# Moving ScalarE's V copy and, every second turn, a set of TensorE transposes in a fused top-k attention and SwiGLU kernel

## The chip, the core and the metric

The kernel runs on one core of a Trainium2 chip. A core has five engines with an instruction queue each: TensorE (PE in the profile, its weight loads shown apart as PEld), VectorE (DVE), ScalarE (ACT), GpSimd (POOL) and SyncE (SP), which here only starts DMA transfers. They meet through semaphores. PE writes to PSUM, a memory of eight banks, from which ACT or DVE must copy the result before the bank can be used again.

The metric is the time of one execution on the device in microseconds (us). The kernel before was timed three times: median 1794.11 us, from 1790.79 to 1795.02.

## What is computed

Top-k attention over 8 batches of 8 heads with 576 tokens of 64 features each, and a SwiGLU feed-forward block on its output, all in fp32. Cut to what matters:

```python
scores = q @ k.T / sqrt(64)                  # 576 x 576 per head
kth    = 32nd largest score of each row
scores = where(scores >= kth, scores, -1e9)
attn   = exp(scores - max);  attn = attn / (sum(attn) + 1e-9)
x      = (attn @ v), heads side by side      # 4608 x 512
out    = (silu(x @ w_gate) * (x @ w_val)) @ w_out   # 512 -> 1536 -> 512
```

## The kernel before

**Units and turns.** The attention is cut into 160 units: for each of 8 batches, five blocks of queries (four of 128, then one of 64), and in each four pairs of heads. A unit of a full block holds two heads (a score tile of 128 x 1152); one of the last block packs 64 queries of both heads into one tile of 128 x 576. The main loop makes one turn per unit (and three more to drain). In turn n several units are in work at different stages, each stage with a line of the listing:

- DVE picks the 32 largest scores of unit n in rounds of eight (`select`, L328 and L332), then writes a penalty for the others (L338). Last in the turn comes the reciprocal of the sums of the unit n-1, whose exp ran in this turn (`normalize`, L371).
- POOL adds penalty and scores of unit n-1 (`penalize`, L348 and L350).
- ACT takes exp of unit n-1 with the row sums (`weigh`, L359 and L364), and scales the unit before it, n-2, by the reciprocal (the rest of `normalize`, L374; the main loop calls it `scaled`).
- PE transposes unit n-2, nine 128 x 128 pieces or five in a one-head unit, into three PSUM banks or two, and ACT copies them to `et` (`turn`, L386 and L387).
- In even turns alone PE computes the scores of units n+1 and n+2 (`scores`, L308, or L294 for one-head units), which ACT copies to `sc` (L313, L299), and between the two the products of `et` with V for units n-4 and n-3 (`values`, L420), which ACT copies to `x` (L436): the V copy. Even turns thus have much attention work on PE, odd turns only the transposes.

The five PSUM banks of the pool `ps_t` go round among scores, products with V, transposes, and the transposes of K and Q (`prep`, L255 to L268).

**The FFN.** The tokens are taken in 18 blocks of 256 (`feed`). A block can begin when all heads of its tokens are in `x`. Its work on PE is handed out in pieces: four 128 x 256 products, each run as two matmuls in fp32 (L476, eight matmuls for one piece), and later pieces of six matmuls for the output product (L562; L522 in the first block). When a product is complete, work for ACT is put on a list `on_act` (tanh, half and add for a gate, L501 to L503; a plain copy for a value, L508) and from there work for POOL on a list `on_pool` (L504, L509). The lists are emptied by `flush` at fixed places of a turn, or by `piece` when they hold more than one entry. The products go round three PSUM banks of the pool `ps_f`.

**Order.** Every engine runs its instructions strictly in the order in which the program writes them: at the end an order dependency is put between each instruction and the one before it on its engine. How many pieces a turn gets follows from a credit (`share`); where in the turn they stand is written out by hand with `pieces(k)`. So the order of calls in the body of the main loop sets everything around the change.

In that body, a turn begins with `flush(on_act)`, `penalize`, `flush(on_pool)`; then comes the scaling (L374), then in even turns the first scores, the products with V and their copy, the second scores on PE, then exp, then the copies of the second scores. Two pieces follow on PE, `flush(on_act)`, and the transposes with their copies, and then the rest of the pieces.

Of the kernel before, what the change touches and what calls it, by code (L numbers as in the profile page):

```python
# [25 lines left out]
def kernel(  # L26
# [174 lines left out]
    def rounding(n):  # L201
        for _ in range(n):
            next(weight, None)
# [70 lines left out]
    def n_heads(qt):  # L274

        return 1 if qt == J else 2

    def scores(n):
        b, qt, hp = units[n]
        slab = preps[b * NHP + hp]  # L280
        sc = work.tile([P, 2 * S], FP32, tag="sc", name="sc", bufs=3)
        halves = [slice(0, D), slice(D, P)]
        half = S // 2

        def bank():
            return ps_t.tile([P, 512], FP32, tag="t", name="s")


        if qt == J:
            banks = [bank() for _ in range(2)]  # L290
            for i, ps in enumerate(banks):
                for d in halves:
                    k0 = R + i * half
                    nc.tensor.matmul(  # L294
                        ps[d, 0:half], slab[d, S + R : S + 2 * R], slab[d, k0 : k0 + half]
                    )
            yield
            for i, ps in enumerate(banks):
                nc.scalar.copy(sc[:, i * half : (i + 1) * half], ps[:, 0:half])  # L299
        else:  # L300
            q0 = S + 2 * R + qt * P
            banks = []
            for i in range(2):
                for hh, d in enumerate(halves):
                    ps = bank()
                    banks.append((i + 2 * hh, ps))
                    k0 = (1 - hh) * R + i * half
                    nc.tensor.matmul(  # L308
                        ps[:, 0:half], slab[d, q0 : q0 + P], slab[d, k0 : k0 + half]
                    )  # L310
            yield
            for i, ps in banks:
                nc.scalar.copy(sc[:, i * half : (i + 1) * half], ps[:, 0:half])  # L313
        state[n] = dict(sc=sc)

    def select(n):

        nh = n_heads(units[n][1])
        sc = state[n]["sc"]
        m = small.tile([P, 2, TOP_K], FP32, tag="m", name="m", bufs=2)  # L320
        heads = [slice(t * S, (t + 1) * S) for t in range(nh)]
        e = work.tile([P, 2 * S], FP32, tag="e", name="e", bufs=3)
        state[n] |= dict(m=m, e=e, heads=heads)
        cur = sc
        rounds = TOP_K // 8
        for r in range(rounds):
            for t, hs in enumerate(heads):
                nc.vector.max(m[:, t, 8 * r : 8 * r + 8], cur[:, hs])  # L328
                yield
            if r < rounds - 1:  # L330
                for t, hs in enumerate(heads):
                    nc.vector.match_replace(  # L332
                        e[:, hs], m[:, t, 8 * r : 8 * r + 8], cur[:, hs], LOWEST
                    )
                    yield
                cur = e
        for t, hs in enumerate(heads):
            nc.vector.tensor_scalar(  # L338
                e[:, hs], sc[:, hs], m[:, t, TOP_K - 1 : TOP_K], FAR, ALU.is_lt, ALU.mult
            )  # L340
# [26 lines left out]
    def normalize(n):  # L367
        st = state[n]
        tot, e, heads = st.pop("tot"), st["e"], st.pop("heads")
        nh = len(heads)  # L370
        nc.vector.reciprocal(tot[:, 0:nh], tot[:, 0:nh])  # L371
        yield
        for t, hs in enumerate(heads):
            nc.scalar.mul(e[:, hs], e[:, hs], tot[:, t : t + 1])  # L374

    def turn(n):

        last = units[n][1] == J
        e = state[n].pop("e")
        et = work.tile([P, 2 * J + 1, P], FP32, tag="et", name="et")  # L380
        for c0, cn in ((0, J), (J, 1)) if last else ((0, J), (J, 1), (J + 1, J)):
            ps = ps_t.tile([P, 512], FP32, tag="t", name="etps")
            kl = R if last and c0 == J else P
            for c in range(cn):
                k0 = (c0 + c) * P
                nc.tensor.transpose(ps[0:kl, c * P : (c + 1) * P], e[:, k0 : k0 + kl], ident[:])  # L386
            nc.scalar.copy(  # L387
                et[0:kl, c0 : c0 + cn, :],
                ps[0:kl, 0 : cn * P].rearrange("p (c j) -> p c j", c=cn),
            )  # L390
            if c0 == J:
                yield
        state[n]["et"] = et
# [64 lines left out]
    def flush(queue):  # L458
        while queue:
            queue.pop(0)()  # L460
# [201 lines left out]
    NU = len(units)  # L662
# [3 lines left out]
    def piece():  # L666

        if len(on_act) > 1:
            flush(on_act)
        if len(on_pool) > 1:  # L670
            flush(on_pool)
        while True:
            if not current:
                if not todo or done.get(todo[0], 0) < NHP * BLK:
                    return 0
                flush(on_act)
                flush(on_pool)
                current.append(feed(todo.pop(0)))
            cost = next(current[0], 0)
            if cost == 0:  # L680
                current.pop()
                continue
            return cost

    def fetch(n):

        b, qt, hp = units[n]
        i = b * NHP + hp
        if qt == 0:
            yield from prep(i)  # L690
        if qt == J and i + NHP < len(pairs):
            load(i + NHP)

    def share(n):


        others = 0.0
        costs = [(m, 0.7) for m in scored(n) + valued(n)] + [(n - TURN, 0.6)]
        for m, cost in costs:
            if m >= 0:  # L700
                others += cost * (0.5 if units[m][1] == J else 1)
        if units[n + 3][1] == 0:
            others += 0.6

        beside = 6.4 if T[1] else 7.0
        return beside * n_heads(units[n][1]) / 2 - others

    def scored(n):

        ahead = [n + 1] if n < 2 else [] if n % 2 else [n + 1, n + 2]  # L710
        return [m for m in ahead if m < NU]

    def valued(n):

        behind = [] if n % 2 else [n - 4, n - 3]
        return [m for m in behind if 0 <= m < NU]

    def pieces(n):
        for _ in range(n):
            if credit[0] >= 1:  # L720
                credit[0] -= piece()

    def run(steps):
        for _ in steps:
            pass

    def finish_units(ns):
        values(ns)
        for n in ns:
            b, qt, hp = units[n]  # L730
            if qt == J and b + 1 < B:
                load_v((b + 1) * NHP + hp)
# [10 lines left out]
    no = iter(())  # L743
    scaled = no
    TURN = 2
    due = [2.0]
    for n in range(NU + 3):
        nh = n_heads(units[n][1]) if n < NU else 1
        topk = select(n) if n < NU else no
        norm = normalize(n - 1) if 0 <= n - 1 < NU else no  # L750
        nxt = [scores(m) for m in scored(n)]
        ahead = fetch(n + 3 if n else 2) if n + 3 < NU else no

        def dve(k, beside=True):

            for _ in range(k * nh):
                next(topk, None)
                due[0] += 5 / 6 if beside else 0
                if due[0] >= 1:
                    due[0] -= 1  # L760
                    rounding(1)

        if n >= NU - NHP:
            credit[0] = 8.0
        else:
            credit[0] = min(credit[0] + share(n), share(n) + 1)
        flush(on_act)
        if 0 <= n - 1 < NU:
            penalize(n - 1)
        flush(on_pool)  # L770
        run(scaled)
        if nxt:
            run(nxt.pop(0))
        if valued(n):
            finish_units(valued(n))
        if nxt:
            next(nxt[0])
        early[0]()
        if 0 <= n - 1 < NU:
            weigh(n - 1)  # L780
        if nxt:
            run(nxt.pop())


        dve(2, beside=False)
        if n == 0:
            run(ahead)
            load(3)
            ahead = fetch(3)
        if n < NHP:  # L790
            load_v(n)
        pieces(2)
        flush(on_act)
        dve(1)
        dve(1)
        if 0 <= n - TURN < NU:
            run(turn(n - TURN))

        flush(on_pool)
        next(ahead, None)  # L800
        pieces(1)
        next(ahead, None)
        dve(1)
        pieces(1)
        dve(2, beside=False)
        run(topk)
        next(norm, None)
        scaled = norm
        pieces(6)
# [50 lines left out]
```

## Time and profile before

| What | Value |
|---|---|
| median of three runs | 1794.11 us |
| the profiled execution's own time | 1794.33 us |
| its span, first to last instruction | 1792.1 us |
| mean granted PE clock | 0.964 |
| PE busy | 1691.1 us, 94% of the span |
| PE weight loads | 1398.6 us, 78% |
| DVE busy | 1619.1 us, 90% |
| ACT busy | 1204.8 us, 67% |
| POOL busy | 1043.2 us, 58% |
| HBM read and written | 48.23 MB and 9.44 MB, 32 GB/s |
| scaling on ACT (L374), each | 780 ns, 288 of them |
| exp on ACT (L359), each | 775 ns, 288 |
| transposes' copies (L387), each | 483 ns, 448 |
| V copy (L436), each | 328 ns, 96 |

Times in the profile are in us from the span's start unless marked ns. The profile gives each instruction's start and duration; a wait is put down to the instruction whose semaphore came last. The ends of PE's matmuls are modelled, so that small pauses inside PE's busy time do not show. Busy shares are means over the span, and this kernel has a start and an end that differ from its middle.

### The profile page before, as it was taken

To read this page: it belongs to the slowest core of one execution; us is meant where nothing else is said; L and a number is where in the kernel's file an instruction comes from. 1 tells how busy PE (TensorE), PEld (TensorE's weight loads), DVE (VectorE), ACT (ScalarE), POOL (GpSimd) and SP (SyncE) were. 2 spreads that over 40 slices of the span, in tenths; PEclk is the share of its full clock that TensorE was granted. 3 is DMA by queue.
4 is the path that set the end of the run, shared out by engine and by line. 5 is a ranking of instruction groups with operands and counts; after the bars stand their busy time and mean duration, and the time that the engine had idled before them with its cause. 6 is when DMAs were issued, how large, how long until landed. Compare 5 with 4: busy or idle time off the path is not lost.

```text
span 1792.1 us, 30800 instructions
## 1 busy us (share of the span) xinstructions
PE 1691.1 (94%) x11012; PEld 1398.6 (78%) x11012; DVE 1619.1 (90%) x3372; ACT 1204.8 (67%) x2881; POOL 1043.2 (58%) x930
## 2 busy tenths in 40 slices
PE   4558999799999999999999999999999999999999
PEld 3337678688888888888888878888887878888877
DVE  7999999999999999998999999998999989999400
ACT  6778676667667676667666675767676676676431
POOL 4878756455565646565556546555556555656434
PEclk7569999899999999999999999999999999999989
DMA  7433130001200030001200020000300020000000
GB/s 193 128 94 94 32 75 14 13 1 36 60 1 13 2 81 14 13 1 32 64 13 1 13 70 26 1 13 4 92 1 13 1 49 21 13 1 13 1 12 12
DMA packets 109305, 59.66 MB, mean 33 GB/s; under 512 B 88544, under 2 KB 96992, under 8 KB 109152
## 3 DMA queue, kind: packets, MB, share of 16 engines
q1 hardware_dynamic: 108016, 57.37, 12.3%
q8 instruction: 87, 1.43, 0.3%
q14 instruction: 66, 0.54, 0.1%
q10 hardware_dynamic: 1136, 0.33, 0.1%
HBM read 48.23 MB, written 9.44 MB: 32 GB/s over the span
## 4 chain that ended last, share of the span: by engine, by line
PE 79%; DVE 12%; ACT 4%; POOL 3%; issue 1%; DMA 1%; SPq 0%; ACTq 0%; POOLq 0%; DVEq 0%
PE f L476 40%; PE x_ps L562 8%; PE av L420 8%; PE s L308 7%; PE etps L386 6%; PE y_ps L562 5%; DVE m L328 5%; DVE e L332 5%; PE s L294 2%; DVE e L338 1%; PE kqps L263 1%; PE o_ps L522 1%; ACT e L359 1%; POOL e L350 1%; DVE size L121 1%
## 5 line engine op out<-in xcount | busy, mean ns | idle before, releaser
L328 DVE MAX8 m<-e 128x8 f32<-128x576 f32 x864 | 614.9, 747 | 3.3
L350 POOL TENSOR_TENSOR e<-e,sc 128x1152 f32<-128x1152 f32 (+1 forms) x160 | 382.9, 2393 | 131.6 <-DVE tot L371 110.0
L332 DVE MATCH_REPLACE8 e<-m,e 128x576 f32<-128x576 f32 x576 | 423.5, 741 | 0.0
L476 PE MATMUL f<-xT,wg 128*128 128x256 f32 x1728 | 403.9, 383 | 0.0
L476 PE MATMUL f<-xT,wv 128*128 128x256 f32 x1728 | 399.6, 380 | 0.0
L476 PEld LDWEIGHTS f<-xT,wg 128*128 128x128 f32 x1728 | 325.2, 192 | 52.0 <-issue 9.2
L476 PEld LDWEIGHTS f<-xT,wv 128*128 128x128 f32 x1728 | 323.0, 190 | 49.1 <-issue 7.9
L504 POOL TENSOR_TENSOR h<-h,half_g 128x512 f32<-128x512 f32 x108 | 139.7, 1293 | 284.8 <-ACT h L503 283.0
L359 ACT ACTIVATE e<-e,bias 128x576 f32<-128x576 f32 x288 | 221.9, 775 | 113.4 <-POOL e L350 113.3
L386 PE MATMUL etps<-ident,e 128*128 128x128 f32 (+1 forms) x1312 | 185.1, 284 | 48.1 <-ACT e L374 33.5
L374 ACT ACTIVATE e<-e,tot 128x576 f32<-128x576 f32 x288 | 210.7, 780 | 22.1 <-DVE tot L371 21.8
L509 POOL TENSOR_TENSOR h<-h,val 128x512 f32<-128x512 f32 x108 | 139.2, 1289 | 148.0 <-ACT val L508 146.9
L386 PEld LDWEIGHTS etps<-ident,e 128*128 128x128 f32 (+1 forms) x1312 | 157.2, 145 | 80.3 <-POOL e L350 30.1
L308 PE MATMUL s<-kqT 64*128 64x288 f32 x1024 | 181.2, 461 | 37.3 <-ACT sc L313 22.0
L332 DVE MATCH_REPLACE8 e<-m,sc 128x576 f32<-128x576 f32 x288 | 211.6, 741 | 0.0
L328 DVE MAX8 m<-sc 128x8 f32<-128x576 f32 x288 | 202.6, 739 | 9.2 <-ACT sc L313 9.2
L387 ACT COPY et<-etps 128x512 f32<-128x512 f32 (+1 forms) x448 | 182.5, 483 | 36.3 <-PE etps L386 36.2
L338 DVE TENSOR_SCALAR e<-sc,m 128x576 f32<-128x576 f32 x288 | 182.8, 671 | 1.2
L313 ACT COPY sc<-s 128x288 f32<-128x288 f32 x512 | 164.8, 407 | 19.0 <-PE s L308 18.7
L308 PEld LDWEIGHTS s<-kqT 64*128 64x128 f32 x1024 | 102.0, 198 | 85.2 <-ACT sc L313 27.3
L420 PE MATMUL av<-et,v 128*64 128x128 f32 (+1 forms) x2560 | 162.6, 271 | 0.0
L420 PEld LDWEIGHTS av<-et,v 128*64 128x64 f32 x2560 | 140.8, 143 | 7.2 <-issue 3.4
(73 smaller groups left out, 1979.3 us busy)
## 6 DMA issues: line engine op xcount, KB each, us to landing
v<-in_v_dram SPq DMA_DIRECT2D x32, 256.0 KB, 3.2
kq_in<-in_k_dram SPq DMA_DIRECT2D x63, 128.0 KB, 3.0
kq_in<-in_q_dram SPq DMA_DIRECT2D x63, 128.0 KB, 3.2
w<-in_moe_w_gate_dram SPq DMA_DIRECT2D x12, 512.0 KB, 3.8
w<-in_moe_w_val_dram SPq DMA_DIRECT2D x12, 512.0 KB, 3.7
w<-in_moe_w_out_dram SPq DMA_DIRECT2D x12, 512.0 KB, 3.6
out_dram<-o SPq DMA_DIRECT2D x38, 128.0 KB, 2.4
out_dram<-o SPq DMA_DIRECT2D x16, 256.0 KB, 2.4
```

Of the source, the lines that this page charges most:

```text
L308: nc.tensor.matmul(ps[:, 0:half], slab[d, q0 : q0 + P], slab[d, k0 : k0 + half])
L328: nc.vector.max(m[:, t, 8 * r : 8 * r + 8], cur[:, hs])
L332: nc.vector.match_replace(e[:, hs], m[:, t, 8 * r : 8 * r + 8], cur[:, hs], LOWEST)
L338: nc.vector.tensor_scalar(e[:, hs], sc[:, hs], m[:, t, TOP_K - 1 : TOP_K], FAR, ALU.is_lt, ALU.mult)
L350: nc.gpsimd.tensor_tensor(e[:, every], e[:, every], sc[:, every], ALU.add)
L359: nc.scalar.activation(e[:, hs], e[:, hs], AF.Exp, bias=bias[:, t : t + 1], scale=scale, accum_out=tot[:, t : t + 1],)
L374: nc.scalar.mul(e[:, hs], e[:, hs], tot[:, t : t + 1])
L386: nc.tensor.transpose(ps[0:kl, c * P : (c + 1) * P], e[:, k0 : k0 + kl], ident[:])
L387: nc.scalar.copy(et[0:kl, c0 : c0 + cn, :], ps[0:kl, 0 : cn * P].rearrange("p (c j) -> p c j", c=cn),)
L420: nc.tensor.matmul(av[d, i, 0:ql], weights_, moving, start=c == (0 if last else J), stop=c == (J if last else J - 1),)
L476: nc.tensor.matmul(ps[:, i, :], w[:, kc, m * P : (m + 1) * P], x[:, kc, :], start=(kc == 0), stop=(kc == KC - 1),)
L562: nc.tensor.matmul(ps, lhsT, T[i][m], start=m == 0, stop=m == MQ - 1)
```

## The change

Two steps move inside the turn. First, `run(scaled)`, the two ACT scalings of unit n-2, stood ahead of the scores and the V copy; it now stands behind the V copy and behind the matmuls of the second scores. On ACT an even turn's order was: scaling, copies of the first scores, V copy, exp, copies of the second scores. It becomes: copies of the first scores, V copy, scaling, exp, copies of the second scores. In odd turns, which have neither scores nor V, the scaling's place among ACT's work is the same.

Second, in odd turns one FFN piece and the whole of `turn(n - 2)`, PE's transposes and ACT's copies of them, now come ahead of exp. Before, two pieces stood between the turn's start and the transposes, and the copies were behind exp and behind the gate or value work of those two pieces. Even turns keep their transposes where they were, behind two pieces. The pieces that follow keep their order, and a turn's total of pieces is the same.

```diff
@@ -768,13 +768,17 @@
         if 0 <= n - 1 < NU:
             penalize(n - 1)
         flush(on_pool)
-        run(scaled)
         if nxt:
             run(nxt.pop(0))
         if valued(n):
             finish_units(valued(n))
         if nxt:
             next(nxt[0])
+        run(scaled)
+        flipped = turn(n - TURN) if 0 <= n - TURN < NU else no
+        if n % 2:
+            pieces(1)
+            run(flipped)
         early[0]()
         if 0 <= n - 1 < NU:
             weigh(n - 1)
@@ -793,8 +797,7 @@
         flush(on_act)
         dve(1)
         dve(1)
-        if 0 <= n - TURN < NU:
-            run(turn(n - TURN))
+        run(flipped)
 
         flush(on_pool)
         next(ahead, None)
```

`TURN` is 2, `nxt` holds the score steps of an even turn, `valued(n)` its two units for the product with V, and `no` is an empty step. `turn` is a generator, so that the second `run(flipped)` does nothing in an odd turn.

## The prediction

> **What bounds the kernel now.** I read the page's busy shares and chain first, then the busy time by stage, then the waits of the part where TensorE (PE) is full, then single turns of the main loop in the timeline. The page, its busy shares and the chain that ended last:
>
> ```profile
> span 1792.1 us, 30800 instructions
> ...
> PE 1691.1 (94%) x11012; PEld 1398.6 (78%) x11012; DVE 1619.1 (90%) x3372; ACT 1204.8 (67%) x2881; POOL 1043.2 (58%) x930
> ...
> PE 79%; DVE 12%; ACT 4%; POOL 3%; issue 1%; DMA 1%; SPq 0%; ACTq 0%; POOLq 0%; DVEq 0%
> ```
>
> Busy time by stretch (length, PE, PEld, DVE, ACT, POOL, then the granted clock):
>
> ```profile
> 140.00:320.00 180.00, 175.75 (x1110) 137.24 (x1107) 177.24 (x350) 133.96 (x315) 123.92 (x101) 0.99 0.18 48
> 320.00:357.00 37.00, 27.26 (x176) 21.19 (x173) 37.00 (x82) 22.26 (x56) 18.09 (x16) 0.79 0.04 15
> 357.00:1690.00 1333.00, 1323.22 (x8857) 1108.94 (x8858) 1268.98 (x2660) 915.90 (x2220) 759.00 (x686) 1.00 0.09 22
> ```
>
> Two regimes. Up to 357 us VectorE (DVE) has no rest: 37.00 of 37 us at the end of it, when FFN blocks 0 and 1 are used up and block 2 still lacks tokens of turn 30. From 357 us to 1690 us PE idles 9.8 of 1333 us. So there a move cannot give much, and every new PE wait is paid in full. Waits on PE after 357 us (total, times, longest):
>
> ```profile
> PE etps L386 <- ACT e L374: 3.7, 1, 3.7
> PE x_ps L562 <- POOL xT L569: 2.7, 2, 2.4
> PE etps L386 <- ACT sc L313: 1.8, 3, 1.5
> ```
>
> The transposes (L386) hardly ever wait for the scaled e (L374) today. What keeps them apart are the two FFN pieces ahead of them. An odd turn, n=63, in the timeline (start, duration):
>
> ```profile
> 683.91 3.62 PE L476 MATMUL f<-xT,wv 128*128 128x256 f32 x16
> 684.12 0.60 ACT L501 ACTIVATE h<-f 128x512 f32<-128x512 f32 x1 [1.03 <-PE f L476]
> ...
> 685.09 0.63 ACT L503 ACTIVATE h<-h 128x512 f32<-128x512 f32 x1
> 685.61 1.44 ACT L374 ACTIVATE e<-e,tot 128x576 f32<-128x576 f32 x2
> 687.37 1.15 PE L386 MATMUL etps<-ident,e 128*128 128x128 f32 x9
> ```
>
> The last product of the even turn ends at 683.9. ScalarE (ACT) then runs its tanh, half and add (L501 to L503), then the scaling. PE covers that with two pieces (3.45 us of weight loads) before the transposes.
>
> **What the skill says.** TensorE: Matmul & The Clock Gate, section "Architectural detail", says that ACT and DVE are strict FIFOs and that PE only pulls weight loads ahead. The trace agrees: at 347.54 and 354.69 us PE stands 0.86 and 2.04 us before score matmuls with other work queued behind. The same page, "What's actually happening", says that the array falls to half clock after an idle window of about 3.4 us. The trace agrees: after the 3.70 us gap at 1718.55 us sixteen FFN matmuls take 5.76 us instead of 3.62. The new waits below are under 3 us each, so I charge no clock loss. Perfetto Trace Analysis, "Per-instruction lifecycle", says that the semaphore's travel is outside the profiled window; here the first scaling ends 0.78 us after its start and a waiting transpose starts 0.91 to 0.92 us after it (n=29, 117, 137), so 0.14 us is the price of the hand-over.
>
> **The change, part by part.** Nothing is added or removed: no instruction, no DMA. DVE's order stays. The moved steps issue no DMA themselves; on SP a few neighbouring loads and stores trade places (DMA landings take 2.4 to 3.8 us, hidden by whole turns). On POOL a gate product (L504 or L509, 1.29 us) sometimes falls behind the next turn's penalty (L350) instead of before it, because it is flushed a piece later: that lets exp start sooner, and PE needs the product blocks later. Both at 0; if the product is wanted for a block's first sum, the waits for POOL above (2.7 us) could grow by about 1 us a block in a few blocks. ACT and PE change inside each turn; the number of pieces per turn stays.
>
> *Odd turns, PE.* The nine transposes come one piece earlier: 1.73 us (L476, eight matmuls) or 1.30 us (L562, six). The scaling in odd turns is where it was, behind the gate work flushed at the turn's start, which itself waits for PE's last product. So this is a loop PE to ACT to PE with one piece of cover less, and PE has nothing else it may run. The first transposes need the first head's scaling, chunk 5 the second's: usable at start of L374 + 1.14 us at full pitch (0.92 where the unit has one head). New wait = that time minus (old start of the transposes minus one piece). n=63: 685.61+1.14 = 686.75 against 687.37-1.73 = 685.64: 1.11 us. Read so from the starts of L374 and L386 in all 66 odd turns from 31 to 161: 37 wait for nothing; eight 0.1, two 0.2, five 0.36, one 0.53, one 0.67, three 0.8, six 1.11, one 1.18, two 1.52 us. Sum 17.4 us. 1.1 us of it (turns 81 and 101) is where DVE's reciprocal ended just before the scaling; as PE falls behind, that goes. Left: +16.3 us.
>
> *Even turns, ACT.* The scaling (1.44 us, 0.78 for one head) goes behind the score copies and the V copy. Both already wait for PE in most turns (the V copy waits 71.8 us for L420 on the page), so they win nothing where PE is full. Exp, the copies of the second score set, the gates and the transposes' copies queue behind the scaling and start up to 1.44 us later where the scaling used to run in an idle stretch. PE's transposes there keep two pieces of cover and need the V copy + 1.4 us: covered, save turns 56 and 116, which have no piece between. In most turns ACT idles over 1 us between exp and the next odd turn's scaling and takes the delay up. In eleven it idles 0.03 to 0.69 us: turns 36, 56, 116 (delays left: 1.0, 1.3, 1.3) and 38, 58, 76, 78, 96, 98, 118, 138 (0.65 each). There the delay reaches the odd turn's scaling and adds to its wait: 3.6 + 5.2 = +8.8 us. Waits for PSUM banks of 0.63 us in six of these even turns, and 0.7 to 0.8 us for the scaling in 56 and 116, fall in the same pairs and are inside this sum: a PE that waited in the even turn waits less in the odd one.
>
> *Odd turns, ACT.* The transposes' copies (1.24 us) go ahead of exp. ACT waits there 97 us for POOL in 52 turns after 300 us, so they are partly free; otherwise exp and its tot come about 1.3 us later, and DVE needs tot only at the turn's end. If that cover is gone, DVE waits and not yet PE. The gate work then follows three pieces instead of two. Three f banks allow it: the bank is asked back four pieces (6.9 us) later, and exp and gate take 1.9 + 1.8 us. Cost: 0.
>
> *Turn 30, the one place for a gain.* Lines from the timeline:
>
> ```profile
> 346.93 1.22 ACT L387 COPY et<-etps 128x512 f32<-128x512 f32 x3
> 347.54 1.49 PE L308 MATMUL s<-kqT 64*128 64x288 f32 x4 [0.86 <-ACT et L387]
> 352.91 1.44 ACT L374 ACTIVATE e<-e,tot 128x576 f32<-128x576 f32 x2 [4.77 <-DVE tot L371]
> 354.69 2.57 PE L308 MATMUL s<-kqT 64*128 64x288 f32 x8 [2.04 <-ACT sc L313]
> ```
>
> PE waits 0.86 us for copies that stood behind exp and 2.04 us for score copies that stood behind a scaling which waited for the reciprocal. Both go: block 2 starts 2.9 us earlier. But turn 30 hangs on DVE, and in turn 16 (V copy ended 221.19, exp started 221.09, reciprocal of its tot at 223.15 with hardly any slack) the scaling now sits before exp: 1.6 us of DVE delay. Net -1.3 us. In the earlier turns tot is ready some 5 us before DVE asks.
>
> *End.* Turn 160's exp waits for POOL until 1719.70 us; the V copy ended at 1718.17, and the last scaling (0.78) fits in between. 0.
>
> Sum: +16.3 + 8.8 - 1.3 = +23.8 us on the profiled 1794.33 us (span 1792.1 and 2.2 around it). The runs' median is 1794.11, so the same sum holds: 1818 us.
>
> **Rivals.**
> *Faster, by ACT's freed time.* ACT's waits in odd turns are filled with copies (up to 1.24 us in 52 turns); if thereby the gates and the next scaling ran early enough that no transposes waited, only turn 30 would count, with the 1.8 us of bank waits: 1794.3 - 2.9 - 1.8 = 1790, down to 1787 if startup waits also shrink. It decides if the scaling ends at least one piece (1.73 us) before the transposes in all odd turns. For it: the idle ACT (67%). Against: the gates wait for PE itself (L501 107.8 us), so ACT cannot get ahead of it.
> *The carry does not happen, and half the short waits are absorbed:* the eight waits of 0.1 and the 0.36 ones vanish, the rest stays: 17.4-1.1-3-1.3 = +12, 1806 us. For it: each is close to what one trace can resolve. Against: the eleven turns without idle ACT.
> *DVE becomes the bound.* Later exp delays tot beyond DVE's reciprocal in eleven even turns (36, 56, 76, 96, 104, 106, 112, 116, 132, 152, 156) by 1.0 to 1.37 us, 13.7 us. If DVE then led, up to 1832 us. For it: DVE is busy 1269 of 1333 us. Against: it already waits 21.1 us for tot there and PE does not notice.
> *No effect:* all waits within what a queue of matmuls hides, and turn 30 swallowed by turn 16: 1794 us.
>
> **Chances.** Main case (1811 to 1825) 0.56, absorbed (1799.5 to 1811) 0.20, DVE bound 0.10, faster 0.09, no effect 0.05. Two repeats of one kernel can't be told apart under 0.3% (5.4 us). Slower 0.86, same 0.05, faster 0.09. Range 1800 to 1829: it leaves out the two last cases and the far end of the DVE case.
>
> **What would show it.** After 357 us the wait of L386 for ACT's e (L374) grows from 3.7 to 20 to 30 us in some 30 odd turns, each 0.1 to 3 us; PE's idle time in 357 to 1690 us from 9.8 to over 30. The wait of L308 for the score copies at 354.69 is gone and FFN of block 2 starts before 357. ACT's wait for POOL before exp shrinks. I am wrong if PE idles no more than before; then the gates must have come earlier than the page shows.

## The result, and the profile after

The changed kernel takes 1820.24 us (median of four runs, 1819.53 to 1820.71), against 1792.71 us for the kernel before in the same comparison: a ratio of 1.0153, 95% interval 1.0135 to 1.017. It is 27.5 us slower; the prediction was 1818 us. The two traces that are compared below are of executions of 1794.33 us (before) and 1820.57 us (changed).

The page of the changed kernel, its span, busy shares and chain:

```profile
span 1818.6 us, 30839 instructions
...
PE 1691.7 (93%) x11012; PEld 1388.8 (76%) x11012; DVE 1630.5 (90%) x3372; ACT 1209.5 (67%) x2881; POOL 1041.4 (57%) x930
...
PE 77%; DVE 9%; ACT 7%; POOL 4%; issue 1%; DMA 1%; SPq 0%; ACTq 0%; POOLq 0%; DVEq 0%
```

PE has the same work, 1691.7 us, in a span 26.5 us longer. The chain's share of ACT has gone from 4% to 7%. The same stretches as before (length, PE, PEld, DVE, ACT, POOL, granted clock):

```profile
140.00:320.00 180.00, 171.64 (x1059) 132.95 (x1059) 171.68 (x342) 128.53 (x301) 123.38 (x100) 0.98 0.18 48
320.00:357.00 37.00, 29.35 (x222) 23.44 (x219) 36.31 (x79) 24.79 (x64) 15.63 (x16) 0.86 0.04 15
357.00:1690.00 1333.00, 1301.92 (x8710) 1079.73 (x8709) 1274.86 (x2649) 909.35 (x2198) 746.99 (x675) 1.00 0.09 22
```

From 357 to 1690 us PE now idles 31.1 us where it idled 9.8. The mean granted clock there is 1.00 in both, so the loss is waiting and not speed. DVE, which had hardly any rest before 357 us, now rests 8.3 us between 140 and 320 us (2.8 before). The largest of PE's waits after 357 us (total, times, longest), and below them one line of the weight loads' waits, up to 1690 us:

```profile
PE etps L386 <- ACT e L374: 7.5, 8, 2.6
PE etps L386 <- issue: 7.3, 7, 2.2
PE etps L386 <- ACT sc L313: 7.2, 7, 2.2
PE x_ps L562 <- POOL h L610: 4.1, 3, 1.6
```

```profile
PEld etps L386 <- ACT e L374: 13.2, 35, 1.0
```

The transposes (L386) stand in front. By name the wait for the scaled e (L374) is only 7.5 us, and 3.6 of it is the last two units, after 1690 us. But many waits are under 1 us and show best on the weight loads: 35 for the scaled e, where the kernel before had 2 (0.5 us). Others carry another releaser's name ("issue", POOL's e), although the scaling is what had just ended. Counted by turn, PE stops over 0.1 us ahead of the transposes in 22 odd turns from 37 to 145, 14.9 us in all (one turn, 1.1 us, before), and in each of them they start 0.05 to 0.15 us after the first scaling has ended. Turn 63, the one shown in the prediction:

```profile
695.48 1.89 PE L476 MATMUL f<-xT,wv 128*128 128x256 f32 x8
695.68 0.60 ACT L501 ACTIVATE h<-f 128x512 f32<-128x512 f32 x1 [1.03 <-PE f L476]
...
696.65 0.63 ACT L503 ACTIVATE h<-h 128x512 f32<-128x512 f32 x1
697.17 1.44 ACT L374 ACTIVATE e<-e,tot 128x576 f32<-128x576 f32 x2
...
698.09 1.34 PE L386 MATMUL etps<-ident,e 128*128 128x128 f32 x9 [0.72 <-POOL e L350]
...
699.95 0.78 ACT L359 ACTIVATE e<-e,bias 128x576 f32<-128x576 f32 x1
```

One piece now covers gate and scaling. PE stops 0.72 us before the transposes, and a little more inside them (1.34 us instead of 1.15, for the second head's scaling); comparing the start of the next even turn's transposes with before, the pair of turns loses 1.09 us. The name "POOL e" is the case of a wait put down to one of several semaphores: the transposes start 0.92 us after the first scaling did.

### The profile page after: what moved, and what is told of

It reads as the page before. It is cut to its first block, busy times and chain, and to the rows that moved or that the text cites. A ratio compares the mean times of both kernels' runs of the same rounds, so it can differ in the third digit from the quotient of the medians.

```text
span 1818.6 us, 30839 instructions
## 1 busy us (share of the span) xinstructions
PE 1691.7 (93%) x11012; PEld 1388.8 (76%) x11012; DVE 1630.5 (90%) x3372; ACT 1209.5 (67%) x2881; POOL 1041.4 (57%) x930
## 4 chain that ended last, share of the span: by engine, by line
PE 77%; DVE 9%; ACT 7%; POOL 4%; issue 1%; DMA 1%; SPq 0%; ACTq 0%; POOLq 0%; DVEq 0%
PE f L476 38%; PE x_ps L562 9%; PE av L420 8%; PE etps L386 7%; PE s L308 6%; PE y_ps L562 5%; DVE m L328 4%; DVE e L332 4%; PE s L294 2%; ACT e L359 1%; ACT e L374 1%; POOL e L350 1%; DVE e L338 1%; PE o_ps L522 1%; PE kqps L263 1%
## 5 line engine op out<-in xcount | busy, mean ns | idle before, releaser
L476 PE MATMUL f<-xT,wg 128*128 128x256 f32 x1728 | 403.6, 383 | 0.0
L476 PE MATMUL f<-xT,wv 128*128 128x256 f32 x1728 | 401.5, 382 | 0.0
L476 PEld LDWEIGHTS f<-xT,wg 128*128 128x128 f32 x1728 | 324.8, 192 | 51.5 <-issue 8.6
L476 PEld LDWEIGHTS f<-xT,wv 128*128 128x128 f32 x1728 | 325.0, 191 | 49.9 <-issue 5.5
L386 PE MATMUL etps<-ident,e 128*128 128x128 f32 (+1 forms) x1312 | 191.7, 288 | 80.9 <-ACT e L374 44.7
L386 PEld LDWEIGHTS etps<-ident,e 128*128 128x128 f32 (+1 forms) x1312 | 156.2, 146 | 125.0 <-POOL e L350 35.5
L387 ACT COPY et<-etps 128x512 f32<-128x512 f32 (+1 forms) x448 | 186.0, 488 | 89.6 <-PE etps L386 86.5
L374 ACT ACTIVATE e<-e,tot 128x576 f32<-128x576 f32 x288 | 211.2, 784 | 10.1 <-DVE tot L371 10.1
L308 PE MATMUL s<-kqT 64*128 64x288 f32 x1024 | 173.3, 453 | 28.0 <-ACT sc L313 20.6
L338 DVE TENSOR_SCALAR e<-sc,m 128x576 f32<-128x576 f32 x288 | 192.4, 704 | 1.1
L420 PE MATMUL av<-et,v 128*64 128x128 f32 (+1 forms) x2560 | 157.4, 266 | 0.0
L308 PEld LDWEIGHTS s<-kqT 64*128 64x128 f32 x1024 | 97.4, 196 | 73.3 <-issue 26.4
L420 PEld LDWEIGHTS av<-et,v 128*64 128x64 f32 x2560 | 135.9, 139 | 7.2 <-ACT kqT L268 2.7
```

Of the source, the lines that this page charges most:

```text
L308: nc.tensor.matmul(ps[:, 0:half], slab[d, q0 : q0 + P], slab[d, k0 : k0 + half])
L338: nc.vector.tensor_scalar(e[:, hs], sc[:, hs], m[:, t, TOP_K - 1 : TOP_K], FAR, ALU.is_lt, ALU.mult)
L387: nc.scalar.copy(et[0:kl, c0 : c0 + cn, :], ps[0:kl, 0 : cn * P].rearrange("p (c j) -> p c j", c=cn),)
L420: nc.tensor.matmul(av[d, i, 0:ql], weights_, moving, start=c == (0 if last else J), stop=c == (J if last else J - 1),)
L476: nc.tensor.matmul(ps[:, i, :], w[:, kc, m * P : (m + 1) * P], x[:, kc, :], start=(kc == 0), stop=(kc == KC - 1),)
```

## The experiments

Two theories were set against each other. Theory A is the prediction's: the transposes have one piece less of cover in a loop PE, gate work and scaling on ACT, PE. Theory B: the copies ahead of exp, and the later scaling in even turns, delay exp, the sums and so DVE, which then leads.

**Each half alone.** The scaling alone, in the main loop:

```diff
         run(scaled)
         flipped = turn(n - TURN) if 0 <= n - TURN < NU else no
-        if n % 2:
-            pieces(1)
-            run(flipped)
         early[0]()
```

> Only the scaling moves behind the V copy; the transposes stay behind two pieces in every turn. Theory A (PE stands in odd turns because the transposes have one piece less of cover in the loop PE, gate work and scaling on ACT, PE; the later scaling of even turns adds to that): with two pieces of cover most of the delay is taken up, so 2 to 8 us slower than before, about 1798 us. Theory B (the copies ahead of exp and the later scaling delay exp, the sums and so DVE, which then leads): about half of the loss stays here, 1803 to 1808 us.

Measured 1798.01 us, ratio 1.0029 (1.0018 to 1.004), as theory A had it.

The transposes alone:

```diff
         flush(on_pool)
+        run(scaled)
         if nxt:
             run(nxt.pop(0))
...
-        run(scaled)
         flipped = turn(n - TURN) if 0 <= n - TURN < NU else no
         if n % 2:
             pieces(1)
             run(flipped)
```

> Only the odd turns change: one piece, transposes and their copies ahead of exp; the scaling of even turns stays first. Theory A: the 17 us of waits read from the trace of before, less about 1 us at turn 30: 1807 to 1811 us, PE's wait of L386 for L374 in some 25 odd turns. Theory B: 1803 to 1808 us with DVE waiting for tot more often than before.

Measured 1813.19 us, ratio 1.0115 (1.01 to 1.013): 2 us above the range of theory A and 5 above B's. The two halves add up to 1.44%, the whole is 1.53% within 1.35 to 1.7%: they are additive within the intervals. The traces tell more than the times. Comparing when the transposes of turn n start with before, even turns only (odd ones start a piece earlier by construction), the scaling alone is 4.3 us *ahead* at turn 30 and 4.7 us behind at turn 158; the transposes alone are 4.2 us behind at turn 30 and 18.6 behind at 158; the changed kernel goes from 1.7 ahead to 27.1 behind. This difference in start is called the lag from here on. From turn 30 to 158 the scaling's move costs 9.0 us, the transposes' 14.4, and both 28.8: 5.4 us more than the halves. Of these 5.4 us, 3.5 arise between turns 30 and 32, where the changed kernel loses 4.3 us, the scaling alone 0.7 and the transposes alone 0.1. From turn 32 on the halves cost 8.3 and 14.3 us and both 24.5, which is 1.9 us more.

**Half clock.** Some of these differences are not waits but speed. In turn 57 PE stops 1.80 us ahead of the transposes both in the changed kernel and in one that is described further down (the scaling ahead of the gates). The first two lines are of the changed kernel, the next two of the other, the last is a stretch of the other:

```profile
644.59 1.38 PE L386 MATMUL etps<-ident,e 128*128 128x128 f32 x9 [1.80 <-issue]
645.80 1.89 PE L476 MATMUL f<-xT,wv 128*128 128x256 f32 x8
```

```profile
643.91 1.38 PE L386 MATMUL etps<-ident,e 128*128 128x128 f32 x9 [1.80 <-issue]
645.13 3.45 PE L476 MATMUL f<-xT,wv 128*128 128x256 f32 x8
```

```profile
645.30:648.71 3.41, 3.41 (x10) 2.61 (x10) 3.20 (x8) 3.17 (x8) 0.14 (x1) 0.50 0.00 0
```

After the same pause the same eight matmuls take 1.89 us once and 3.45 us once, at a granted clock of 0.50. Between 370 and 1690 us the traces have 17 such stretches, each 3.41 us long: one before (turn 102, after a pause of 2.36 us), one in the changed kernel (turn 137), one with the transposes alone (turn 56), three in the one just shown, one with the transposes moved from turn 33 on, ten in the run without cover, none with the scaling alone or with PE's order alone. One costs about 1.5 us; this is an estimate from the pair above and from turn 102 before, where twelve matmuls take 4.38 us (the same twelve take 2.86 us in the trace of the last kernel below, after a pause of 2.33 us). The pauses around them are 1.80 to 3.62 us long, and in the 3.41 us ahead of each PE was busy for 15 to 47%. Other pauses of this length were not followed by half clock; what decides it is not shown. Counted with 1.5 us each, the 1.9 us above shrink to some 0.4: from turn 32 on the halves add up.

**PE's order or ACT's?** The transposes' half is split again. With the copies alone moved, PE's order is that of before:

```diff
         if n % 2:
-            pieces(1)
+            pieces(2)
             run(flipped)
...
-        pieces(2)
+        if n % 2 == 0:
+            pieces(2)
```

(against the transposes alone).

> In odd turns the transposes stay behind two pieces on PE, so PE's order is that of before; only ACT's copies of them go ahead of exp. Theory A: no cover is lost, so within 3 us of before (1790 to 1796 us). Theory B: the copies delay exp and the gates, so most of what the transposes' half of the change costs is here, 1800 us or more.

Measured 1814.27 us, ratio 1.012 (1.0102 to 1.0138). Theory A said 1790 to 1796: it missed, and theory B's 1800 or more came. The four executions spread from 1809.73 to 1817.48 us, and the trace is of the fastest. The other split, PE's transposes one piece earlier with the copies where they were (all of a unit's transposes are issued first, its copies in a second step):

```diff
         if n % 2:
             pieces(1)
-            run(flipped)
+            next(flipped, None)
...
-            nc.scalar.copy(
-                et[0:kl, c0 : c0 + cn, :],
-                ps[0:kl, 0 : cn * P].rearrange("p (c j) -> p c j", c=cn),
-            )
-            if c0 == J:
-                yield
+            made.append((c0, cn, kl, ps))
+        yield
+        for c0, cn, kl, ps in made:
+            nc.scalar.copy(
+                et[0:kl, c0 : c0 + cn, :],
+                ps[0:kl, 0 : cn * P].rearrange("p (c j) -> p c j", c=cn),
+            )
```

> In odd turns PE transposes one piece earlier as in the changed kernel, but ACT copies them where it did before, behind exp and the gates. Theory A: the whole loss of the transposes' half is here, 1806 to 1812 us. Theory B: about as before, 1790 to 1797 us.

Measured 1809.79 us, ratio 1.0097 (1.0081 to 1.0114), as theory A had it. The split is not quite clean: in 25 of the 79 odd turns one more gate or value now stands ahead of the copies on ACT than before, since a third piece precedes them. So PE's earlier transposes cost about 17 us with the copies behind exp, and some 3 us more with them ahead. But copies ahead of exp cost 21 us when the transposes stay behind two pieces. The copies-alone trace says why; its waits on PE after 357 us begin with work that has nothing to do with the transposes, the copies of the transposed K and Q (`kqT`):

```profile
PE s L308 <- ACT kqT L268: 6.1, 5, 2.1
PE av L420 <- ACT kqT L268: 5.2, 3, 1.7
```

and a piece of its timeline at a batch's end:

```profile
850.76 1.25 ACT L387 COPY et<-etps 128x512 f32<-128x512 f32 x3 [1.86 <-PE etps L386]
...
851.88 0.80 ACT L359 ACTIVATE e<-e,bias 128x576 f32<-128x576 f32 x1
...
854.48 0.58 ACT L268 COPY kqT<-kqps 128x512 f32<-128x512 f32 x1
...
855.11 0.44 PE L420 MATMUL av<-et,vlast 128*64 128x128 f32 x4 [1.74 <-ACT kqT L268]
```

There ACT waits for transposes that stand behind two pieces, exp waits behind their copies, then gate and `kqT` copies behind exp, and PE waits. The product `av` (L420) does not read `kqT`, so there it is the PSUM bank that it waits for; for the scores (L308), which do read it, bank and data are not told apart. The reciprocals of this kernel are 3.8 us late by turn 29 as well. So the two orders are not two independent items: copies ahead of exp are cheap only if the transposes come early, and early transposes have a piece less of cover. Theory B is right about the copies-alone kernel up to turn 30, where DVE's delay is carried on; after that, PE waiting for the `kqT` copies (11.3 us in the two lines above) is what its trace shows.

**The dose.** If the loop is what PE waits for, taking the second piece away as well must cost what the trace of before says:

```diff
         if n % 2:
-            pieces(1)
             next(flipped, None)
```

(against the kernel with PE's order alone).

> As the run with PE's order alone, but in odd turns the transposes come ahead of all pieces: two pieces of cover less than before. Theory A (the loop PE, gate work, scaling, PE): the waits read from the trace of before with two pieces taken off sum to 84 us in 57 of 66 odd turns, so with some 3 us at the start 1870 to 1885 us. If a wait is bounded by something else than the scaling, or if the earlier reciprocals let the scaling start sooner as PE falls behind, the loss is at most about double that of one piece, 1825 to 1835 us.

Measured 1894.46 us, ratio 1.0567 (1.0552 to 1.0583), 10 us above theory A's range and far from doubling. In its trace (where L387 are the transposes) PE's wait for the scaling from 357 to 1792 us, and the stretch to 1690 us:

```profile
PE etps L387 <- ACT e L374: 49.5, 33, 4.6
```

```profile
357.00:1690.00 1333.00, 1265.02 (x8331) 1045.21 (x8332) 1212.85 (x2543) 868.28 (x2108) 701.81 (x639) 0.98 0.09 22
```

PE idles 68 us there. From turn 32 to 158 the lag grows from 14.0 to 98.1 us, by 84.1, where 84 had been read from the trace of before. That the sums agree so closely is luck; the turns tell more. In 40 of the 63 odd turns from 33 to 157, and in 34 of the 54 of them that were to wait at all, the lag that a turn adds is within 0.15 us of the reading. Nine turns (39, 59, 63, 79, 89, 99, 117, 119, 137) add 1.2 to 1.7 us more than was read, 13.6 us in all, and around the transposes of each a stretch at half clock begins; the tenth stretch is at turn 57. Thirteen turns add 10.7 us less, 4.3 of them at turn 101, behind which the kernel before has its own pause and half clock. So the waits themselves come to about 70 us, an estimate: 84.1 less ten times 1.5, plus the 1.5 that before lost at turn 102. The time missed the range because 14.0 us are lost by turn 32, where 3 were set.

**What holds the scaling.** In odd turns the scaling goes ahead of the gate and value work, once on the kernel with PE's order alone and once on the changed kernel:

```diff
+        if n % 2:
+            run(scaled)
         flush(on_act)
         if 0 <= n - 1 < NU:
             penalize(n - 1)
```

> As the run with PE's order alone (one piece of cover less), but in odd turns the scaling goes ahead of the gate and value work that is flushed at the turn's start. Theory A: the waits behind gates and values (9.0 of the 17.4 us read from the trace of before) go, those behind the transposes' and prep copies stay: 1799 to 1803 us against 1809.8. If the gate work is not what holds the scaling, no change: 1808 to 1812 us.

Measured 1801.01 us, ratio 1.0044 (1.0029 to 1.006): 8.8 us less by the medians than with PE's order alone, where 9.0 was expected.

> The changed kernel, with the scaling in odd turns ahead of the gate and value work. Theory A: about 9 us of the 27 come back: 1809 to 1813 us. Otherwise 1818 to 1823 us.

Measured 1815.49 us, ratio 1.0118 (1.0104 to 1.0132): 4.7 us come back by the medians, about half of what was expected. Turn 63 in this kernel:

```profile
696.37 1.45 ACT L374 ACTIVATE e<-e,tot 128x576 f32<-128x576 f32 x2 [0.70 <-DVE tot L371]
696.50 1.89 PE L476 MATMUL f<-xT,wv 128*128 128x256 f32 x8
697.72 0.57 ACT L501 ACTIVATE h<-f 128x512 f32<-128x512 f32 x1
698.23 1.15 PE L386 MATMUL etps<-ident,e 128*128 128x128 f32 x9
```

The scaling now waits for DVE's reciprocal, 1.9 us ahead of the transposes, and PE no longer stops. That is so in turns 63, 67, 69, 89, 95 and 115 alike: from turn 62 to 70 the changed kernel loses 3.3 us and this one nothing. Most of what is missing is lost again to half clock: at the pauses of turns 57 and 117 (1.80 and 2.23 us, as long as in the changed kernel) this trace has two stretches that the changed kernel's trace has not, and they cost 1.6 us each. So from turn 54 to 62 this kernel loses 5.7 us and the changed one 4.0. Without them some 7.9 us would have come back, near the 9 expected (an estimate: 4.7 and twice 1.6).

**The start.** The kernel with the transposes alone, moved up to turn 31 only:

```diff
-        if n % 2:
+        if n % 2 and n < 32:
             pieces(1)
             run(flipped)
```

> The transposes and copies are moved in odd turns up to 31 only, the scaling stays first everywhere. If VectorE's delay in turns 13 to 28 is passed on whole to the start of block 2: 2.5 to 4.5 us slower than before, 1795.5 to 1797.5 us. If PE's idle time before block 2 swallows it: 1791 to 1794 us.

Measured 1794.57 us, ratio 1.0016 (1.0006 to 1.0025), nine runs from 1794.01 to 1797.63. That is 2.9 us by the ratio; the median lies 0.9 us under the range and 0.6 over the one for a swallowed delay. The nine runs form two groups, five from 1794.01 to 1794.57 and four from 1796.82 to 1797.63, and the trace is of the upper one (1797.55): there DVE's reciprocal of turn 29 is 3.6 us late, and the lag is 4.9 us at turn 30. What parts the groups is not known, so that the delay is passed on is shown for the upper one alone.

The changed kernel, with the transposes moved from turn 33 on only:

```diff
-        if n % 2:
+        if n % 2 and n >= 32:
             pieces(1)
             run(flipped)
```

> The changed kernel, but the transposes and their copies are moved in odd turns from turn 33 on only; the scaling is moved everywhere. If the part of the loss that the prediction did not have (some 6 us between turns 30 and 36) comes from VectorE being late at turn 30 because the copies ahead of exp delay the sums in turns 13 to 28, the block starts 4 us earlier than before at turn 30 and this loss goes: 1813 to 1817 us against 1820. If those waits belong to the turns after 32 themselves: 1818 to 1821 us.

Measured 1815.62 us, ratio 1.0132 (1.0115 to 1.0149), in the range of the first reading. At turn 30 it is 4.2 us ahead of before and at turn 158 21.7 behind, where the changed kernel is 27.1 behind. But the loss between turns 30 and 36 goes only in part: 3.8 us of it stay, of 6.5 in the changed kernel.

**A version that is faster than both.** The scaling behind the V copy in turns 0 to 31 alone:

```diff
         flush(on_pool)
-        run(scaled)
+        if n >= 32:
+            run(scaled)
         if nxt:
             run(nxt.pop(0))
...
+        run(scaled)
         early[0]()
```

(against the kernel before; the second call does nothing where the first has run).

> The scaling goes behind the V copy in turns 0 to 31 alone; from turn 32 on everything is as before. If the gain of the scaling's move sits at turn 30, where block 2 waits for the V copy, and its loss in the later even turns, this keeps the gain of about 4 us that the single-part run shows at turn 30: 1788 to 1790 us, faster than both kernels. If the gain is swallowed later, 1792 to 1795 us.

Measured 1790.1 us in 19 runs, ratio 0.9984 (0.9977 to 0.9991): 2.8 us faster than before by medians, 0.1 us above the expected range. Turn 30 in its timeline:

```profile
352.56 1.24 PE L308 MATMUL s<-kqT 64*128 64x288 f32 x8
352.68 0.43 ACT L436 COPY xT<-av 128x128 f32<-128x128 f32 x2 [2.94 <-PE av L420]
353.04 1.44 ACT L374 ACTIVATE e<-e,tot 128x576 f32<-128x576 f32 x2
353.73 3.72 PE L476 MATMUL f<-xT,wg 128*128 128x256 f32 x16
```

The wait of 2.04 us for the score copies is gone, and block 2 of the FFN begins at 353.73 us instead of 357.19. This is the gain that the change holds. With the scaling moved in all turns (the first run above) it is used up by turn 78.

## Why the prediction was right, and where it was not

**The bound.** PE full after 357 us, and new PE waits paid there: right. Its idle time there rose by 21.3 us, to 31.1 ("over 30" was written), and the span by 26.5; the rest is 4.6 us more idle time before 357 us and 0.6 us of busy time.

**Odd turns on PE, +16.3 us.** The mechanism is shown three ways: PE's order alone costs 17 us in time; of the odd turns from 33 to 157 that were to wait, 18 of 27 with PE's order alone and 34 of 54 without cover add to the lag what was read, within 0.15 us; and the scaling ahead of the gates returns 8.8 of the 9.0 us put down to them. The size was read too high: PE's order alone loses only 11.3 us from turn 32 to 158, or some 12.8 without the 1.5 us of half clock that the kernel before has at turn 102. The waits of 0.1 us did show (0.07 to 0.08 each), so the rival that has the short waits absorbed did not come. The 1.2 us read for turn 57 and 0.5 for turn 145 did not show; the wait of turn 81, which the prediction took off as bound by the reciprocal, did (0.33 us). And some delay was hidden behind waits that the kernel before had itself, as at turn 102, where the block of the kernel before waits 2.4 us for POOL and that of this one 1.3. Another 4.1 us had been lost by turn 32, which the step did not contain (the traced executions of the two kernels are 15.3 us apart).

**The scaling of even turns, +8.8 us.** Turns and size were named rightly: alone, the scaling loses 8.3 us from turn 32 to 158 (some 9.8 without the half clock of before), and 8.0 us of it in the places named, 34 to 40, 56 to 60, 76 to 80, 96 to 100, 116 to 120 and 138. The way was right in part. That kernel keeps its two pieces of cover, so the loss should mostly have been taken up; it comes as bank waits of 0.71 us in six of the even turns (the prediction had 0.63) and as longer waits of the K and Q transposes (L263) for ACT's copies, and hardly in odd turns (0.9 us at 117). At the starts of FFN blocks, where the prediction named a growth and put it at 0, L562 of the changed kernel waits for POOL 7.4 us after 357 us instead of 4.2.

**Copies ahead of exp, cost 0.** Not quite: 3.4 us between the medians of the transposes alone and of PE's order alone, whose intervals overlap. In the trace most of it falls at turn 56, where the lag of the first jumps by 3.8 us and that of the second by none: the first waits 1.86 us for POOL before L562, and one stretch at half clock follows. Gate work behind exp comes late, as the sentence on POOL had allowed for; the half clock was not foreseen. That the copies' cost is not a number of its own, but 21 us behind two pieces, was nowhere in the prediction.

**No clock loss.** The prediction charged none because its waits are under 3 us. From turn 32 to 158 this cost the changed kernel nothing on balance, since its trace has one stretch at half clock there and that of the kernel before has one too. But the assumption does not hold here: of the 17 stretches, 16 stand at pauses under 3 us, and without cover they come to some 15 us (ten times the 1.5 above).

**Turn 30, -1.3 us.** The step that failed. The waits of 0.86 and 2.04 us did go, and the transposes of turn 30 start 1.7 us earlier. But DVE's delay is 4.4 us and not 1.6. Turn 16 of the changed kernel:

```profile
223.01 0.37 ACT L436 COPY xT<-av 128x256 f32<-128x256 f32 x1 [1.94 <-PE av L420]
223.28 1.44 ACT L374 ACTIVATE e<-e,tot 128x576 f32<-128x576 f32 x2
224.62 0.76 ACT L359 ACTIVATE e<-e,bias 128x576 f32<-128x576 f32 x1
226.59 0.17 DVE L371 RECIPROCAL tot<-tot 128x2 f32<-128x2 f32 x1 [4.77 <-ACT tot L364]
```

The place was right, and that the scaling sits in front of exp. That the V copy itself comes 2.2 us later, since PE had already lost that time at the transposes of turns 11 and 13, was left out: early odd turns were taken as free because PE idles later. The single parts bear this out: the scaling alone leaves the reciprocal of turn 29 where it was, the transposes alone make it 2.7 us late, both together 4.4. And what follows was missed. Turn 30 in the changed kernel:

```profile
356.09 3.72 PE L476 MATMUL f<-xT,wg 128*128 128x256 f32 x16
359.64 0.60 PE L386 MATMUL etps<-ident,e 128*128 128x128 f32 x4
360.11 0.77 ACT L359 ACTIVATE e<-e,bias 128x576 f32<-128x576 f32 x1 [1.31 <-POOL e L350]
361.97 1.28 ACT L313 COPY sc<-s 128x288 f32<-128x288 f32 x4
362.40 0.96 PE L386 MATMUL etps<-ident,e 128*128 128x128 f32 x5 [2.15 <-ACT sc L313]
```

Block 2 begins 1.1 us earlier, but exp is held by POOL, which is held by the late DVE; the score copies come behind it, and PE waits 2.15 us for a bank. Half clock follows (0.50 from 363.44 to 366.86 us), and the next eight matmuls (L476) take 3.37 us instead of 1.89. The lag goes from 1.7 us ahead to 2.6 behind in two turns. Moving the transposes from turn 33 on only, which spares DVE the delay, returns 4.6 us by the medians.

**The end, 0,** held: the pauses around the last transposes are 1.04 and 2.60 us instead of one of 3.70.

**The rivals.** Faster needed the scaling to lead the transposes by a piece everywhere, and it did not. DVE as the bound did not come: from 357 to 1690 us PE idles 31 us and DVE rests 58 us.

**The sum.** The total loss of 27.5 us is 3.7 above the sum of 23.8, and closer than its terms, which is partly luck. The traces give +2.6 us at turn 32 (-1.3 foreseen), then 11.3 for PE's order (16.3), 3.0 for the copies (0), and 8.3 and 1.9 for the scaling alone and together with the rest (8.8): 27.1 us at turn 158. The odd turns were set too high; the start and the copies too low.

## What to carry to other kernels

Where one engine is full, look at what covers each hand-over that goes out from it and comes back to it. Taking one piece of cover away costs the piece's length less the slack, and that can be read from one trace: here most turns came out within 0.15 us, and the sums some 20 to 30% too high. Look at the granted clock as well as at the waits, since a pause can cost more than its length. An order that is good where another engine leads (here the scaling behind the V copy, up to turn 31) can be bad where this one leads, and a program that writes its order by hand can have both. Moving copies ahead on an in-order queue is not free by itself: it makes everything behind wait for what the copies wait for.

## What was not expected of the hardware

Half clock came after short pauses. Without cover there were ten stretches of 3.41 us at a granted clock of 0.50, at pauses of 1.86 to 3.62 us; and the same pause of 1.80 us in turn 57 was followed by it in one kernel and not in another.

With PE's own order unchanged, moving three copies (1.24 us) on ACT's queue in odd turns cost 21 us (1.012, 1.0102 to 1.0138). PE's busy time hides part of such a loss: the same 1312 transposes show 185.1 us in the kernel before and 191.7 in the changed one, with the same mean clock (0.964 and 0.965); a group that stops in its middle, as at 698.09 us above, still counts as busy.
